# Decode block on one core: one head's softmax ahead of a loop, and the last product in column form

## The chip, the cores and the metric

The kernel runs on one core of a Trainium2 chip. The metric is the device time of one execution in microseconds (us). Three runs of the kernel before gave 355.38, 355.39 and 355.53 us, so its median is 355.39 us. The profile is of a further execution, which took 355.74 us.

## The reference, cut to what matters

One token goes through a block of attention over a cache of keys and values, and then through a feed-forward layer. Both are modulated by a vector c (shift, scale and gate; the rows of `mod` below).

```python
mod = (_silu(c) @ w_mod)                     # sa, ca, ga, sb, cb, gb: 512 numbers each
h = _layernorm(x) * (1 + ca) + sa
x = x + ga * _A_ref(h, k_cache, v_cache, wq, wo)
h = _layernorm(x) * (1 + cb) + sb
x = x + gb * (jnp.maximum(h @ w1, 0) @ w2)

def _A_ref(x, k_cache, v_cache, wq, wo):     # 32 query heads, 8 key/value heads, 32768 positions, Dh = 128
    q = x @ wq
    scores = einsum(q, k_cache) * Dh ** -0.5
    o = einsum(softmax(scores), v_cache)
    return o @ wo
```

All inputs are bf16. The caches are 2 x 64 MB; w_mod is 3 MB, wq and wo are 4 MB each, and w1 and w2 are 1.75 MB each (512 x 1792).

## The kernel before, in words

**Loads.** Every large input goes through a ring of five buffers of 4 MB in SBUF. One queue, SP's, issues all the loads in a fixed order (`stream`, lines 139 to 144): w_mod, wq, the keys of head 0, then in turn half a head's keys of the next head and half a head's values of the current one, at the end the values of head 7 in three parts, wo in four, w1 in two and w2 in six. A load can be issued when its buffer is free again and when the transfer that used its semaphore before has landed.

**Scores.** For a key/value head g, the 32768 positions are four steps (u = 0 to 3) of 64 positions for each of 128 partitions; a load brings two steps. `turn_k` (line 405, VectorE) turns 32x32 blocks of the keys in place, in halves of a step, and `scores` (line 422, TensorE) multiplies them, eight matmuls for a half step, into a PSUM bank that collects two steps. `bank_max` (line 428) copies a full bank to SBUF and takes its maximum.

**Softmax.** `softmax(h)` is a Python generator, so that its pieces can be put between other work; each `next(soft)` emits one piece: (1) the maximum over both banks, `m_p`; (2) its transpose on TensorE, `mT_ps`; (3) `Mrow` and `Mexp` on VectorE; (4) a second transpose `Mb_ps` on TensorE, then on ScalarE `nbias` and the exponentials `P_g`; (5) the turned `PT_g` and `Lexp` on VectorE; (6) the matmul `L_ps`; (7) its reciprocal `Linv`.

**Values.** `pv(g, us)` multiplies the turned P by the values of two steps. For heads 0 to 5, and for the first half of head 6, it is a hardware loop on TensorE (lines 490 to 496), 32 matmuls in eight turns; a loop is a section of its own, and the instructions of all engines are divided by it into those ahead of it and those behind it. The second half of head 6 and all of head 7 are written out. `open_o`, `blocks`, `o_cols` and `normalise` clear, fold, turn and scale a head's output.

**Order.** TensorE's and VectorE's orders are as written (line 599); the other engines' are chosen by the scheduler. The loop of lines 611 to 664 works on two heads: the scores of head h = g + 1 and the values of head g. In its turn g = 5 it does the scores of head 6, piece 1 of head 6's softmax, the loop over the second half of head 5's values, and piece 2. Pieces 3 to 7 stand in the turn g = 6 between the first scores of head 7:

```python
            build_qbd(h)
            turn_k(h, 0, 0); turn_k(h, 0, 1); turn_k(h, 1, 0)     # one a line in the kernel
            scores(h, 0, 0)
            if soft:
                next(soft)
            open_o(g)
            scores(h, 0, 1)
```

**End.** `project` multiplies by wo: its last two parts in column form (lines 566 to 572), where a 128x128 piece of the weights is the stationary operand and one column of the activations moves. Then come the second layernorm and the product with w1 in rows (`hid_ps`, line 714), which is transposed on VectorE (line 724); a ReLU on ScalarE (line 725) spreads it over `hid_bd`, 4x4 diagonal blocks. The product with w2 (line 735) is in row form: the stationary operand is 128x4 of `hid_bd`, 128 columns of w2 move, 56 matmuls, and the result is 4 partitions of 128 numbers. For the last step the gate gb and the residual x1 must lie in the same form; `expand` (line 323) and `four_rows` (line 330) make it, gb near the start (line 340) and x1 inside the second layernorm (`meanwhile`, line 698). `keep_clock(n)` issues n matmuls whose result nobody reads. The output goes from 4 partitions to memory (line 743).

Of the kernel before, what the change touches and what calls it, by code (L numbers as in the profile page):

```python
# [9 lines left out]
BF16 = mybir.dt.bfloat16  # L10
F32 = mybir.dt.float32
ACT = mybir.ActivationFunctionType
ALU = mybir.AluOpType
AX = mybir.AxisListType
# [3 lines left out]
def kernel(  # L18
# [14 lines left out]
    nc = tc.nc  # L33
    P = 128
    _, _, D = A_x.shape
# [3 lines left out]
    KT = D // P  # L39
    Dff = B_w1.shape[1]  # L40
    FT = Dff // P
# [142 lines left out]
    for n in sorted({n * REP for _, n in WOP}):  # L184
# [21 lines left out]
    nc.vector.tensor_reduce(  # L206
        out=place32[:], in_=ident_f[:].rearrange("p (j m) -> p m j", m=32), op=ALU.add, axis=AX.X,
    )
    rowpick = const.tile([P, KT], F32)
    nc.vector.tensor_reduce(  # L210
        out=rowpick[:], in_=ident_f[:].rearrange("p (j m) -> p j m", m=32), op=ALU.add, axis=AX.X,
    )
    hid_bd = const.tile([P, FT, KT, KT], BF16)
    nc.gpsimd.memset(hid_bd[:], 0.0)

    pick8 = const.tile([16, 8], BF16)
    nc.vector.tensor_tensor(out=pick8[:], in0=ident_bf[0:16, 0:8], in1=ident_bf[0:16, 8:16], op=ALU.add)
# [22 lines left out]
    def bank(name):  # L240
        return ps_s.tile([P, 512], F32, tag="s", name=name)[:]
# [75 lines left out]
    for i in range(2):  # L317
# [1 line left out]
            mod_rows[:, i, :].rearrange("q (m ko) -> q ko m", ko=KT),  # L319
            modT_sb[:, 4 * KT * i:4 * KT * (i + 1)].rearrange("p (j ko) -> p j ko", j=4),  # L320
        )

    def expand(src_T, name):
        e = const.tile([P, 32, KT], F32, name=f"{name}_exp")
        nc.vector.tensor_tensor(
            out=e[:], in0=src_T.unsqueeze(1).to_broadcast([P, 32, KT]),
            in1=place32[:].unsqueeze(2).to_broadcast([P, 32, KT]), op=ALU.mult,
        )
        return e

    def four_rows(e, name):

        r_ps = bank(f"{name}_ps")[0:KT, 0:P]
        nc.tensor.matmul(  # L334
            r_ps, lhsT=rowpick[:], rhs=e[:].rearrange("p m kt -> p (m kt)"), start=True, stop=True,
        )
        return r_ps

    gb_rows = const.tile([KT, P], F32)
    nc.scalar.copy(out=gb_rows[:], in_=four_rows(expand(modT_sb[:, 5 * KT:6 * KT], "gb"), "gb"))  # L340

    hT = const.tile([P, KT], BF16)
    stat1 = const.tile([P, 2], F32)
# [35 lines left out]
    def build_qbd(g):  # L379
        d_ap = qbd[g % 2][:]  # L380
        d_ps = d_ap.ap[0][0]
        s_ap = qrep_sb[:]
        s_ps = s_ap.ap[0][0]
        for a in range(4):
            o = AP(d_ap.tensor, d_ap.offset + (32 * a) * d_ps + 4 * 7 + 32 * a,
                   [[d_ps, 32], [QW, 4], [1, 4]])
            i = AP(s_ap.tensor, s_ap.offset + (32 * a) * s_ps + REP * g,
                   [[s_ps, 32], [Hq, 4], [1, 4]])
            nc.scalar.copy(out=o, in_=i)  # L389
# [202 lines left out]
    def keep_clock(n):  # L592

        if not spare:
            spare.append(bank("spare_ps"))
        for _ in range(n):
            nc.tensor.matmul(spare[0], lhsT=ident_bf[:], rhs=qbd[0][:, :, 0:P], start=True, stop=True)  # L597

    with tc.manual_schedule(engines={mybir.EngineType.PE, mybir.EngineType.DVE}):
        build_qbd(0)  # L600
        for u in range(NTILE):
            for half in range(2):
                turn_k(0, u, half)
                scores(0, u, half)
            if u % 2 == 1:
                bank_max(0, u // 2)
        soft = softmax(0)
        for _ in soft:
            pass
        soft = None  # L610
        for g in range(LAST):
            h = g + 1
            build_qbd(h)
            turn_k(h, 0, 0)
            turn_k(h, 0, 1)
            turn_k(h, 1, 0)
            scores(h, 0, 0)
            if soft:
                next(soft)
# [4 lines that stand above are left out]
            if g > 0:  # L624
                blocks(g - 1)
            scores(h, 1, 0)
            if g > 0:
                o_cols(g - 1)
            turn_k(h, 1, 1)
            scores(h, 1, 1)  # L630
            if soft:
                next(soft)
            if g > 0:
                normalise(g - 1)
                if g in [sum(w) for w in WOP]:
                    spread(part_of(g - 1))
            if soft:
                next(soft)
            bank_max(h, 0)
            next(soft or iter(()), None)  # L640
            pv(g, (0, 1))
            for u in (2, 3):
                for half in range(2):
                    turn_k(h, u, half)
                    scores(h, u, half)
            bank_max(h, 1)
            soft = softmax(h)
            next(soft)
            if g < LOOPED:
                pv(g, (2, 3))  # L650
                next(soft)
                continue
            next(soft)
            next(soft)
            pv(g, (2,), range(6))
            next(soft)
            next(soft)
            open_o(LAST)
            pv(g, (2,), range(6, 16))
            pv(g, (3,))  # L660
            next(soft)
            next(soft, None)
            a_rows.append(row_bank("a_ps"))
            blocks(g)
        pv(LAST, (0, 1))
        o_cols(LAST - 1)
        normalise(LAST - 1)
        pv(LAST, (2,))
        spread(2)
        hid_ps = ps_o.tile([P, 512], F32, tag="o", name="hid_ps")  # L670
        nc.vector.memset(hid_ps[:], 0.0)
        pv(LAST, (3,))
        blocks(LAST)
        project(0)
        keep_clock(2)
        o_cols(LAST)
        keep_clock(2)
        project(1)
        normalise(LAST)
        spread(3)  # L680
        keep_clock(2)
        project(2)
        keep_clock(1)
        join_rows()
        keep_clock(2)
        project(3)


        stat2 = const.tile([P, 2], F32)
        x1T = const.tile([P, KT], F32)  # L690
        nc.vector.tensor_tensor(out=x1T[:], in0=attnT_ps, in1=modT_sb[:, 2 * KT:3 * KT], op=ALU.mult)
        nc.vector.scalar_tensor_tensor(
            out=x1T[:], in0=x1T[:], scalar=1.0, in1=xT, op0=ALU.mult, op1=ALU.add, accum_out=stat2[:, 0:1],
        )
        h2T = const.tile([P, KT], BF16)
        x1_ps = []

        def meanwhile():
            e = expand(x1T[:], "x1")
            keep_clock(2)  # L700
            x1_ps.append(four_rows(e, "x1"))
            keep_clock(2)

        keep_clock(3)
        layernorm_T(x1T[:], stat2, h2T[:], modT_sb[:, 3 * KT:4 * KT], ncb[:], "ln2", meanwhile)
        x1_rows = const.tile([KT, P], F32)
        nc.vector.tensor_copy(out=x1_rows[:], in_=x1_ps[0])

        NQ = 32 * FT
        for part, (k0, k1) in enumerate(W1P):  # L710
            w1_sb = need(("w1", part))
            for kt in range(k0, k1):
                for q in range(4):
                    nc.tensor.matmul(  # L714
                        hid_ps[32 * q:32 * q + 1, 0:NQ], lhsT=h2T[:, kt:kt + 1],
                        rhs=w1_sb[:, kt - k0, q * NQ:(q + 1) * NQ], start=False, stop=(kt == KT - 1),
                        skip_group_check=True,
                    )
        keep_clock(3)
        hidT = rows_sb("hidT").rearrange("p a b -> p (a b)")[:, 0:NQ].rearrange("p (f e) -> p f e", e=32)  # L720
        hid_v = hid_ps[:, 0:NQ].rearrange("p (e f) -> p f e", f=FT)
        hb = hid_bd[:]
        for f0, f1 in ((0, FT // 2), (FT // 2, FT)):
            nc.vector.transpose(out=hidT[:, f0:f1], in_=hid_v[:, f0:f1])  # L724
            nc.scalar.activation(
                out=AP(hb.tensor, hb.offset + KT * KT * f0, [hb.ap[0], [KT * KT, f1 - f0], [KT + 1, KT]]),
                in_=hidT[:, f0:f1, 0:1].to_broadcast([P, f1 - f0, KT]), func=ACT.Relu,
            )

        ffn_ps = bank("ffn_ps")[0:KT, 0:P]  # L730
        for part, (f0, f1) in enumerate(W2P):
            w2_sb = need(("w2", part))
            for ft in range(f0, f1):
                for i in range(KT):
                    nc.tensor.matmul(  # L735
                        ffn_ps, lhsT=hid_bd[:, ft, i, :], rhs=w2_sb[:, ft - f0, i * P:(i + 1) * P],
                        start=(ft == 0 and i == 0), stop=(ft == FT - 1 and i == KT - 1),
                    )
        o_rows = const.tile([KT, P], F32)
        nc.vector.tensor_tensor(out=o_rows[:], in0=ffn_ps, in1=gb_rows[:], op=ALU.mult)  # L740
        o_bf = const.tile([KT, P], BF16)
        nc.vector.tensor_tensor(out=o_bf[:], in0=o_rows[:], in1=x1_rows[:], op=ALU.add)
    nc.sync.dma_start(out=out[0, 0].rearrange("(i n) -> i n", i=KT), in_=o_bf[:])


# [28 lines left out]
```

## Time and profile before

| | |
|---|---|
| median of three runs | 355.39 us (355.38 to 355.53) |
| profiled execution | 355.74 us, of which its span, first to last instruction, 353.94 us |
| TensorE matmuls busy | 279.8 us (79%) |
| VectorE busy | 203.1 us (57%) |
| ScalarE busy | 25.4 us (7%) |
| read from memory | 149.42 MB, 422 GB/s over the span |
| mean granted TensorE clock | 0.947 |

PE is TensorE's matmuls, PEld its weight loads, DVE is VectorE, ACT ScalarE, POOL GpSimd, and SPq the queue of the loads; L735 is line 735 of the kernel. A line of the timeline gives the start, the duration, the engine, the line, the operation and the tiles; in brackets stands the engine's idle time before it, and what ended it. A line of the chain of work that ended last gives the start, the duration and the instruction. A line of the windows gives a stretch, its length, the busy time and number of instructions of PE, PEld, DVE, ACT and POOL, the granted clock, the share of time that the transfers were busy, and GB/s.

The transfers are at work from 1.8 us on, and the last piece of w2 lands at 350.5 us. The output's transfer is issued at 351.84 us and has landed at 353.02 us; the rest of the span is the end of the program.

### The profile page before, as it was taken

To read this page: it belongs to the slowest core of one execution; us is meant where nothing else is said; L and a number is where in the kernel's file an instruction comes from. 1 tells how busy PE (TensorE), PEld (TensorE's weight loads), DVE (VectorE), ACT (ScalarE), POOL (GpSimd) and SP (SyncE) were. 2 spreads that over 40 slices of the span, in tenths; PEclk is the share of its full clock that TensorE was granted. 3 is DMA by queue.
4 is the path that set the end of the run, shared out by engine and by line. 5 is a ranking of instruction groups with operands and counts; after the bars stand their busy time and mean duration, and the time that the engine had idled before them with its cause. 6 is when DMAs were issued, how large, how long until landed. Compare 5 with 4: busy or idle time off the path is not lost. (4 is left out here: it accounts for less than half of the span.)

```text
span 353.9 us, 4006 instructions
## 1 busy us (share of the span) xinstructions
PE 279.8 (79%) x1311; PEld 112.7 (32%) x1311; DVE 203.1 (57%) x271; ACT 25.4 (7%) x69; POOL 3.9 (1%) x16
## 2 busy tenths in 40 slices
PE   0542781999898979897979796979689687989996
PEld 0221230333343323332323232323234233334444
DVE  6245775882768268462939178553938095734142
ACT  1220003000010001000100001000100010002000
POOL 4000000000000000000000000000000000000000
PEclk9995997799899999998999899999999997999999
DMA  8999999999999999999999999999999999999994
GB/s 309 455 422 445 431 422 441 441 418 424 459 418 422 459 418 424 441 437 426 433 444 417 430 456 419 427 446 426 422 448 430 422 439 441 422 430 424 421 420 177
DMA packets 6852, 149.59 MB, mean 423 GB/s; under 512 B 824, under 2 KB 1080, under 8 KB 1976
## 3 DMA queue, kind: packets, MB, share of 16 engines
q1 hardware_dynamic: 6776, 149.43, 98.4%
q8 instruction: 8, 0.13, 0.1%
q14 instruction: 4, 0.03, 0.0%
q0 software_dynamic: 64, 0.00, 0.0%
HBM read 149.42 MB, written 0.00 MB: 422 GB/s over the span
## 5 line engine op out<-in xcount | busy, mean ns | idle before, releaser
L405 DVE STREAM_TRANSPOSE Ksb<-Ksb 128x2048 f32<-128x2048 f32 x64 | 142.9, 2281 | 63.9 <-DMA Ksb<-in_A_k_cache_dram 63.9
L484 PE MATMUL o_ps<-Vsb,PT_g 128*16 (+1 forms) x512 | 130.0, 395 | 21.5 <-ACT qbd L389 7.2
L422 PE MATMUL S_ps<-Ksb,qbd 128*128 128x512 bf16 x512 | 121.8, 388 | 23.5 <-DVE Ksb L405 21.9
L422 PEld LDWEIGHTS <-qbd 128*128 128x128 bf16 x512 | 49.0, 98 | 87.6 <-issue 31.8
L484 PEld LDWEIGHTS o_ps<-Vsb,PT_g 128*16 x416 | 37.4, 90 | 90.2 <-issue 63.7
L428 DVE TENSOR_SCALAR_CACHE_REDUCE S_g<-S_ps 128x512 f32<-128x512 f32 x16 | 11.0, 690 | 34.4 <-PE S_ps L422 34.4
L389 ACT COPY qbd<-qrep_sb 32x16 bf16<-32x16 bf16 x32 | 6.4, 201 | 138.7 <-PE S_ps L422 137.6
L465 DVE STREAM_TRANSPOSE PT_g<-P_g 128x1024 bf16<-128x1024 bf16 x8 | 9.7, 1218 | 6.6 <-ACT P_g L459 6.6
L484 PEld LDWEIGHTS <-PT_g 128*16 128x16 bf16 x96 | 8.2, 90 | 11.0
L456 ACT ACTIVATE nbias<-Mb_ps 128x1 f32<-128x1 f32 x8 | 1.4, 171 | 136.8 <-PE Mb_ps L454 136.8
L459 ACT ACTIVATE P_g<-S_g,nbias 128x1024 bf16<-128x1024 f32 x8 | 9.2, 1148 | 0.2
L227 PE MATMUL xc_ps<-cx_sel,cx_bd 16*128 16x2 bf16 x4 | 0.3, 172 | 11.1 <-DVE cx_bd L221 11.1
L515 DVE SCALAR_TENSOR_TENSOR Y<-o_ps,smask,Y 16x128 f32<-16x128 f32 x24 | 8.1, 339 | 0.8
L471 PE MATMUL L_ps<-Lexp,ones_f 128*128 128x4 f32 x16 | 3.0, 257 | 4.3 <-DVE Lexp L468 4.3
L597 PE MATMUL spare_ps<-qbd,ident_bf 128*128 128x512 bf16 x19 | 5.6, 380 | 0.0
L440 PE MATMUL mT_ps<-ident_f,m_p 128*1 128x128 f32 x8 | 2.2, 270 | 3.9 <-DVE m_p L437 2.0
L471 PEld LDWEIGHTS L_ps<-Lexp,ones_f 128*128 128x128 f32 x16 | 3.1, 221 | 5.8 <-issue 5.1
L443 DVE TENSOR_REDUCE Mrow<-mT_ps 1x4 f32<-1x128 f32 x8 | 2.1, 257 | 4.6 <-PE mT_ps L440 4.6
L534 DVE TENSOR_TENSOR oT_sb<-acc_ps,Linv 128x4 bf16<-128x4 f32 x8 | 1.2, 150 | 5.7 <-PE acc_ps L521 5.7
L295 PE MATMUL mod_ps<-wm_sb,siluT 128*1 128x512 bf16 x24 | 3.6, 624 | 1.0 <-DVE siluT L289 1.0
L505 DVE MEMSET o_ps<- 16x512 f32 x8 | 3.9, 485 | 0.8
L552 DVE CAST o_sb<-o_ps 128x4 bf16<-128x4 f32 (+2 forms) x4 | 0.7, 167 | 5.7 <-PE o_ps L548 5.7
(115 smaller groups left out, 80.0 us busy)
## 6 DMA issues: line engine op xcount, KB each, us to landing
Ksb<-in_A_k_cache_dram SPq DMA_DIRECT2D x16, 4096.0 KB, 35.6
Vsb<-in_A_v_cache_dram SPq DMA_DIRECT2D x15, 4096.0 KB, 35.2
wq_sb<-in_A_wq_dram SPq DMA_DIRECT2D x1, 4096.0 KB, 19.6
Vsb<-in_A_v_cache_dram SPq DMA_DIRECT2D x2, 2048.0 KB, 31.8
wm_sb<-in_w_mod_dram SPq DMA_DIRECT2D x1, 3072.0 KB, 10.4
wo_sb<-in_A_wo_dram SPq DMA_DIRECT2D x1, 2048.0 KB, 29.1
w_sb<-in_B_w_dram SPq DMA_DIRECT2D x1, 1344.0 KB
wo_sb<-in_A_wo_dram SPq DMA_DIRECT2D x1, 1024.0 KB, 31.1
```

What stands on the lines that cost most here:

```text
L295: nc.tensor.matmul(dst[j // 4][32 * (j % 4):32 * (j % 4) + 1, :], lhsT=src_T[:, kt:kt + 1], rhs=w[:, kt, j * 512:(j + 1) * 512], start=(kt ...
L389: nc.scalar.copy(out=o, in_=i)
L405: t = nc.vector.transpose(out=KTt.bitcast(F32), in_=KTt.bitcast(F32))
L422: nc.tensor.matmul(S_ps_tiles[g], lhsT=qbd[g % 2][:, hp, 4 * (7 - s):4 * (7 - s) + P], rhs=KTv[:, 16 * sl:16 * sl + 16, h, :, par], start= ...
L428: nc.vector.tensor_scalar(out=S_tiles[g][:, G, :], in0=S_ps_tiles[g], scalar1=1.0, scalar2=None, op0=ALU.mult, op1=ALU.max, accum_out=m_ti ...
L459: nc.scalar.activation(out=P_g[:], in_=S_g[:].rearrange("p g f -> p (g f)"), func=ACT.Exp, bias=nbias[:], scale=scale, accum_out=l_g[:],)
L465: nc.vector.transpose(out=PT_g[:], in_=P_g[:])
L471: nc.tensor.matmul(L_ps[:], lhsT=ones_f[:], rhs=Lexp[:], start=True, stop=True)
L484: nc.tensor.matmul(o_tiles[g][:], lhsT=PT, rhs=Vx, start=False, stop=False, skip_group_check=True)
L505: nc.vector.memset(o_tiles[g][:], 0.0)
L515: nc.vector.scalar_tensor_tensor(out=Y[:], in0=o[:, s], scalar=smask[:, s:s + 1], in1=Y[:], op0=ALU.mult, op1=ALU.add,)
L597: nc.tensor.matmul(spare[0], lhsT=ident_bf[:], rhs=qbd[0][:, :, 0:P], start=True, stop=True)
```

## The change

It has two parts.

The first moves softmax pieces of head 6. In the turn g = 5, pieces 2 to 5 (up to the turned P and `Lexp`) now stand ahead of the loop over the second half of head 5's values, and piece 6 behind it. In the turn g = 6 piece 7 comes right after the turned keys; all four half steps of head 7's first keys are turned first and their scores follow one another.

The second writes the last product in column form. The 128x128 pieces of w2 are stationary, and one column of `hid` (128 x 14) moves, 56 matmuls of one column each into four columns of a PSUM tile that VectorE clears beforehand. The gate and the residual are then used as they are, 128x4. So `expand`, `four_rows`, `rowpick`, `gb_rows`, `x1_rows` and `hid_bd` go; in the layernorm the two pairs of `keep_clock` matmuls with the x1 matmul between them become five `keep_clock` matmuls; the ReLU writes 128x7 twice and not 128x28 twice. The output is stored from 128 partitions, 8 bytes of each, and not from 4 partitions, 256 bytes of each.

```diff
-    rowpick = const.tile([P, KT], F32)
-    nc.vector.tensor_reduce(out=rowpick[:], ...)
-    hid_bd = const.tile([P, FT, KT, KT], BF16)
-    nc.gpsimd.memset(hid_bd[:], 0.0)
...
-    def expand(src_T, name):
-    def four_rows(e, name):
-    gb_rows = const.tile([KT, P], F32)
-    nc.scalar.copy(out=gb_rows[:], in_=four_rows(expand(modT_sb[:, 5 * KT:6 * KT], "gb"), "gb"))
...
+            ahead = h == LAST
             build_qbd(h)
             turn_k(h, 0, 0)
             turn_k(h, 0, 1)
             turn_k(h, 1, 0)
+            if ahead:
+                turn_k(h, 1, 1)
+                next(soft, None)
+                soft = None
             scores(h, 0, 0)
...
             scores(h, 1, 0)
+            if ahead:
+                scores(h, 1, 1)
             if g > 0:
                 o_cols(g - 1)
-            turn_k(h, 1, 1)
-            scores(h, 1, 1)
+            if not ahead:
+                turn_k(h, 1, 1)
+                scores(h, 1, 1)
...
             soft = softmax(h)
             next(soft)
+            if g == LOOPED - 1:
+                for _ in range(4):
+                    next(soft)
             if g < LOOPED:
                 pv(g, (2, 3))
                 next(soft)
...
-        layernorm_T(x1T[:], stat2, h2T[:], modT_sb[:, 3 * KT:4 * KT], ncb[:], "ln2", meanwhile)
-        x1_rows = const.tile([KT, P], F32)
-        nc.vector.tensor_copy(out=x1_rows[:], in_=x1_ps[0])
+        layernorm_T(x1T[:], stat2, h2T[:], modT_sb[:, 3 * KT:4 * KT], ncb[:], "ln2", lambda: keep_clock(5))
+        ffn_ps = bank("ffn_ps")[:, 0:KT]
+        nc.vector.memset(ffn_ps, 0.0)
+        hid = const.tile([P, FT], BF16)
...
+            nc.scalar.activation(out=hid[:, f0:f1], in_=hidT[:, f0:f1, 0], func=ACT.Relu)
...
-                for i in range(KT):
+                for ko in range(KT):
                     nc.tensor.matmul(
-                        ffn_ps, lhsT=hid_bd[:, ft, i, :], rhs=w2_sb[:, ft - f0, i * P:(i + 1) * P],
-                        start=(ft == 0 and i == 0), stop=(ft == FT - 1 and i == KT - 1),
+                        ffn_ps[:, ko:ko + 1], lhsT=w2_sb[:, ft - f0, :].rearrange("p (m ko) -> p ko m", ko=KT)[:, ko, :],
+                        rhs=hid[:, ft:ft + 1], start=False, stop=(ft == FT - 1), skip_group_check=True,
                     )
...
+        o_T = const.tile([P, KT], F32)
+        nc.vector.tensor_tensor(out=o_T[:], in0=ffn_ps, in1=modT_sb[:, 5 * KT:6 * KT], op=ALU.mult)
+        o_bf = const.tile([P, KT], BF16)
+        nc.vector.tensor_tensor(out=o_bf[:], in0=o_T[:], in1=x1T[:], op=ALU.add)
+    nc.sync.dma_start(out=out[0, 0].rearrange("(p k) -> p k", k=KT), in_=o_bf[:])
```

More of the change, by code (lines that the diff above doesn't have):

```diff
@@ L208 @@
     )
-    rowpick = const.tile([P, KT], F32)
-    nc.vector.tensor_reduce(
-        out=rowpick[:], in_=ident_f[:].rearrange("p (j m) -> p j m", m=32), op=ALU.add, axis=AX.X,
-    )
-    hid_bd = const.tile([P, FT, KT, KT], BF16)
-    nc.gpsimd.memset(hid_bd[:], 0.0)
     pick8 = const.tile([16, 8], BF16)
@@ L321 @@
         )
-    def expand(src_T, name):
[L324 to L329, printed above, removed]
-    def four_rows(e, name):
[L333 to L337, printed above, removed]
-    gb_rows = const.tile([KT, P], F32)
-    nc.scalar.copy(out=gb_rows[:], in_=four_rows(expand(modT_sb[:, 5 * KT:6 * KT], "gb"), "gb"))
     hT = const.tile([P, KT], BF16)
@@ L695 @@
         h2T = const.tile([P, KT], BF16)
[L696 to L702, printed above, removed]
         keep_clock(3)
-        layernorm_T(x1T[:], stat2, h2T[:], modT_sb[:, 3 * KT:4 * KT], ncb[:], "ln2", meanwhile)
-        x1_rows = const.tile([KT, P], F32)
-        nc.vector.tensor_copy(out=x1_rows[:], in_=x1_ps[0])
+        layernorm_T(x1T[:], stat2, h2T[:], modT_sb[:, 3 * KT:4 * KT], ncb[:], "ln2", lambda: keep_clock(5))
+        ffn_ps = bank("ffn_ps")[:, 0:KT]
+        nc.vector.memset(ffn_ps, 0.0)
+        hid = const.tile([P, FT], BF16)
         NQ = 32 * FT
@@ L721 @@
         hid_v = hid_ps[:, 0:NQ].rearrange("p (e f) -> p f e", f=FT)
-        hb = hid_bd[:]
         for f0, f1 in ((0, FT // 2), (FT // 2, FT)):
             nc.vector.transpose(out=hidT[:, f0:f1], in_=hid_v[:, f0:f1])
[L725 to L730, printed above, removed]
+            nc.scalar.activation(out=hid[:, f0:f1], in_=hidT[:, f0:f1, 0], func=ACT.Relu)
         for part, (f0, f1) in enumerate(W2P):
@@ L733 @@
             for ft in range(f0, f1):
-                for i in range(KT):
+                for ko in range(KT):
                     nc.tensor.matmul(
-                        ffn_ps, lhsT=hid_bd[:, ft, i, :], rhs=w2_sb[:, ft - f0, i * P:(i + 1) * P],
-                        start=(ft == 0 and i == 0), stop=(ft == FT - 1 and i == KT - 1),
-                    )
[L739 to L743, printed above, removed]
+                        ffn_ps[:, ko:ko + 1], lhsT=w2_sb[:, ft - f0, :].rearrange("p (m ko) -> p ko m", ko=KT)[:, ko, :],
+                        rhs=hid[:, ft:ft + 1], start=False, stop=(ft == FT - 1), skip_group_check=True,
+                    )
+        o_T = const.tile([P, KT], F32)
[3 more added lines that the diff above has]
+    nc.sync.dma_start(out=out[0, 0].rearrange("(p k) -> p k", k=KT), in_=o_bf[:])
 _INS = ['A_x', 'A_k_cache', 'A_v_cache', 'A_wq', 'A_wo', 'B_x', 'B_w1', 'B_w2', 'c', 'w_mod']
```

## The prediction

> **What bounds the kernel now.** I read the page's slices first. Apart from the first and the last, the transfers' row holds nines throughout.
>
> ```profile
> DMA  8999999999999999999999999999999999999994
> ```
>
> So the loads set the pace, and engine time counts only where it ends after the last load it needs. The windows show where that happens:
>
> ```profile
> 320.00:330.00 10.00, 10.00 (x48) 4.25 (x47) 2.89 (x9) 0.46 (x1) 0.00 (x0) 1.00 0.97 413
> ...
> 345.00:350.00 5.00, 4.88 (x63) 2.82 (x62) 1.64 (x7) 0.80 (x3) 0.00 (x0) 1.00 0.82 318
> ```
>
> Towards the end PE (second figure) has no idle time either. PE and the transfers run side by side, and the chain of work that ended last names PE:
>
> ```profile
> 343.25 0.50 PE acc_ps L567 x16
> ...
> 346.10 0.94 PE hid_ps L714 x16
> ...
> 347.89 3.30 PE ffn_ps L735 x56
> ...
> 351.22 0.29 DVE o_rows L740
> ...
> 351.53 0.28 DVE o_bf L742
> ```
>
> The last product takes 3.30 us, 59 ns a matmul by this row, and runs to 351.19. When had its last operand landed? Of SP's loads, the last was issued at 341.81:
>
> ```profile
> L132 SPq DMA_DIRECT2D w_sb<-in_B_w_dram x1: 328/328/328, 341.8 to 341.8; - x1
> ...
> DMA to landing us min/median/max: 8.7/8.7/8.7
> ```
>
> It landed at 350.5, only 0.7 before the product's end. This is the number that decides: whatever PE gains beyond it, the last four matmuls cannot start before 350.5.
>
> The moved softmax lies at 275 us. The timeline there, around the two loops it touches:
>
> ```profile
> 275.82 0.15 DVE L437 TENSOR_REDUCE m_p<-m 128x1 f32<-128x2 f32 x1
> 276.84 0.57 PEld L484 LDWEIGHTS o_ps<-Vsb,PT_g 128*16 x4 [2.29 <-issue]
> 276.87 1.02 PE L484 MATMUL o_ps<-Vsb,PT_g 128*16 x4 [1.82 <-issue]
> ...
> 298.65 8.94 PE L484 MATMUL o_ps<-Vsb,PT_g 128*16 x32 [0.66 <-PE L_ps L471]
> ```
>
> The first loop starts 0.90 after `m_p` ends, though it does not read `m_p`. The list of waits confirms that a loop waits for work whose result it does not use:
>
> ```profile
> PE o_ps L484 <- ACT qbd L389: 7.2, 4, 1.8
> ```
>
> **The change part by part.** The sum is made against the profiled execution: 355.74, span 353.94, 1.80 outside it. The median of the runs is 0.35 lower than that execution.
>
> *Last product.* Row form costs 59 ns a matmul. Column form stands in the trace in the same shape, 128x128 weights and one moving column: L567, 16 in 0.50, 31 ns a pair. So 56 take 1.75 instead of 3.30. Started at 347.89 it would be through at 349.64, but the last piece lands at 350.5. Hence: 350.52 landing, 0.05 until the load starts (as `acc_ps` L521 starts 0.04 after `Y` ends), 0.18 for the first pair (the `o_ps` matmul L548), three more at 0.03, 0.04 to DVE: `o_T` starts at 350.88 instead of 351.22. Gain 0.34, not 1.55. The other 52 pairs need 1.6 and would be done at 349.5, so PE may come 1.05 later than today without moving the end; I call that the slack.
>
> *Last two DVE operations.* 0.28 each in 4x128; in 128x4 the same kind (L691, L692) takes 0.16, starts 0.20 apart. Gain 0.24.
>
> *The store.* Before: issued at 351.84, landed at 353.02, 0.83 after the issue's end; its four 256-byte packets took 15 ns each, and the semaphores landed 0.33 after them. The issue costs the same (0.35; loads of 128 rows 0.33). After: 128 pieces of 8 bytes, eight for each of 16 engines. Nothing in the trace has this shape. From below: no change, as all packets are short (4 bytes: 9 ns), less the 6 ns that each is shorter. Nearest row: the first load of 128 rows, wm, had its first packets 0.65 to 0.91 after its issue, the store 0.43; plus eight packets at 9 ns. From above: eight landings in series, 7 x 0.33 = 2.3. I take +0.2, by the load. The Trainium skill ("DMA: Bandwidth & Descriptors", Specifications) says that transfers below 512 B are read, modified and written; no row here prices that, and it would push towards the upper end.
>
> *ReLU, x1, gb.* The ReLU of 128x28 takes 0.27, the cast of 128x16 (L370) 0.22: 0.05, hidden by the landing. In the layernorm, PE's x1 matmuls (0.31) give way to one more `keep_clock` matmul (0.22), and DVE's `x_exp` and `x_rows` (0.28, 0.27) to a memset of some 0.07. None was on the path: `h2T` ends at 346.03, and w1's last part lands at 346.05 (322.24 plus 23.8), so `hid_ps` could not end much earlier anyway. At the start go `rowpick` (DVE 0.27), `gb_exp` (DVE 0.29), two matmuls (0.38), an ACT copy (0.26) and POOL's last memset (0.30); nothing queues behind the last. wq lands at 20.8 and the first keys at 30.5, and the transfers do not pause: worth nothing. Were that cover gone, it would be 0.3 to 0.6.
>
> *The moved softmax.* Ahead of the loop PE now waits at `Mb_ps` for DVE's `Mrow` and `Mexp`; behind it on PE are the loop's 32 matmuls, `L_ps` and head 7's scores. Head 7's own chain has the durations: `mT_ps` 0.27, `Mrow` 0.28, `Mexp` 0.21. From `m_p` at 275.82 that puts `Mb_ps` at 276.9; with a loop entry of 1.3 (idle before L484: 0.7 to 1.8) the loop starts at 278.3, 1.4 later than now. `P_g` on ACT (1.15) and `PT_g` on DVE (1.25) then run beside it; DVE is free until the keys that it turns at 283.51. PE's longer idle time can bring the half clock: in the windows, 292.23 to 295.65 has PE busy for 1.69 of 3.42, and the next two show a granted clock of 0.50. At half clock a matmul of this loop starts every 0.43, so it can lose up to 2. The loop ends between 287.7 and 289.7 (now 286.28). In return head 7's first scores run as one block: now 286.6 to 297.4 with a gap of 1.73 and the half clock; after, 32 in 7.1 as at 307.78, the last eight not before the fourth turn is through at 292.4. With `o_cols`, `normalise`, `spread` and the entry (2.0) the next loop starts between 297.4 and 299.5; now it does at 298.65. So PE comes to the last heads between 1.2 earlier and 0.9 later. Earlier buys nothing (the landing), later fits the slack. SP's next load waits for the loop's end (286.45) but lands 35.8 after its issue: a delay of 3 is hidden. Worth 0.
>
> *Sum.* -0.34 - 0.24 + 0.2 = -0.38: span 353.56, execution 355.36, median 355.0. No change within 0.2% (0.71 us), which is about what a measurement of this kernel can tell.
>
> **The rivals.**
>
> *The loop waits for the turned P too (slower).* If the loop waits for all that is written ahead of it, as for `m_p` and the qbd copies, it waits for `Lexp`, which in head 7's chain ends 4.9 after `m_p` starts, 0.75 of that spent behind other matmuls. It would start at 280.9, 4.0 later, lose 1 to 2 to the half clock, and the unbroken scores give back 2 to 3: the next loop starts 2.5 to 3.5 late. Above the slack of 1.05, 1.4 to 2.4 reach the end: 356.4 to 357.4. Against: the loop at 298.65 began before `Linv`, written ahead of it, had been waited for in full; `bank_max` was still running at 298.39, 0.03 before its first turn was set up. From a delay of 1.4 on the time is above the old one, from 2.1 on by 0.2%. Chance 0.2.
>
> *The store is dear (slower).* More than 1.1 over the old one, up to 2.3: 355.9 to 357.1. Chance 0.05.
>
> *The transfers end earlier than I count (faster).* 349.96 was when 15 of the 16 engines had delivered the last piece; if the sixteenth keeps up, 0.55 more is gained, and if the store costs nothing extra 0.2 more: 354.3. With no transfer in the way at all the product alone would give 1.55 and the time would be 353.8. Against: the transfers are full from 2 us on, and the amount of data is the same. Chance 0.1.
>
> *Column form is no faster than row form.* At 59 ns a pair it ends where it did; 0.24 less, 0.2 more: 355.4. L567 speaks against it. Chance 0.05.
>
> *The weight loads do not overlap (slower).* One 128-column load takes 118 ns (L567, median); 56 in series are 6.6, 3.3 more than now: 358.6. The row refutes it: those loads start every 31 ns. Chance 0.02. The Trainium skill ("TensorE: Matmul & The Clock Gate", LDWEIGHTS) gives the columns over 1.2 as a load's nanoseconds, 107 for 128, against 3 for the 4 columns of today; by that alone 56 would be an estimated 6.0 and the time an estimated 358.0. The trace agrees with the duration and not with such a sum.
>
> **How the numbers follow.** My forecast has 0.58, its own range 354.7 to 355.7 (the store without an extra, or with one of 0.9). Faster: 0.1. Slower: 0.2 + 0.05 + 0.02 = 0.27. Within 0.2%: 0.58 + 0.05 = 0.63. The range goes from 354.4 to 357.0: it takes in most of the earlier landing, and half of the late loop.
>
> **What would show it.** Right: `ffn_ps` in groups with idle time between them, released by w2's loads; the last four starting just after 350.5; `o_T` and `o_bf` at 0.16; the store 0.83 to 1.1 after its issue. The loop over head 5's second half starts near 278.3 and `PT_g` runs beside it. Wrong: that loop starts only after `Lexp`, near 281, and `ffn_ps` is one unbroken row ending after 351.2; or the last load lands well before 350; or the store lands later than 1.5 after its issue.

## The result

The changed kernel takes 356.66 us (356.50 to 357.07), the kernel before on the same chip 355.42 us (355.29 to 355.53). The ratio is 1.0035, with a 95% interval of 1.0024 to 1.0047: 1.24 us slower. The prediction was 355.0 us and no change; the time lies inside its range, on the side to which it gave 0.27.

The profiled execution after took 356.75 us, its span 354.97, which is 1.03 longer than the span before. The transfers' row of the slices is as full as it was:

```profile
DMA  8999999999999999999999999999999999999993
```

The windows, as before, for the long middle and for the last product (length, then busy time of PE, PEld, DVE, ACT, POOL, the granted clock, the transfers' share, GB/s):

```profile
320.00:330.00 10.00, 10.00 (x47) 4.08 (x45) 2.34 (x7) 0.00 (x0) 0.00 (x0) 1.00 0.98 416
345.00:350.00 5.00, 4.09 (x70) 2.46 (x69) 1.15 (x5) 0.43 (x2) 0.00 (x0) 1.00 0.83 321
```

In the last stretch PE now has 0.9 us of idle time where it had 0.1. What it waits for stands in PE's list of waits (total, times, longest), and the chain that ended last agrees:

```profile
PE ffn_ps L709 <- DMA w_sb<-in_B_w_dram: 0.7, 2, 0.4
```

```profile
341.59 8.70 DMA w_sb<-in_B_w_dram
...
350.33 0.31 PE ffn_ps L709 x4
...
350.66 0.17 DVE o_T L714
...
350.86 0.16 DVE o_bf L716
```

So up to the last sum the change loses nothing: the last piece of w2 lands at 350.29, four matmuls follow, and the store is issued at 351.05, 0.79 us earlier than before. The loss is behind that. Below are the store's issue in the kernel before, its issue and landing in the changed kernel, and then SP's wait for it at the end, first in the kernel before and then in the changed one (the numbers behind DMA_DIRECT2D are the issue's duration in ns and its start):

```profile
L743 SPq DMA_DIRECT2D out_dram<-o_bf x1: 348/348/348, 351.8 to 351.8; - x1
```

```profile
L717 SPq DMA_DIRECT2D out_dram<-o_bf x1: 347/347/347, 351.1 to 351.1; - x1
...
DMA to landing us min/median/max: 3.0/3.0/3.0
```

```profile
SPq L769 <- DMA out_dram<-o_bf: 0.4, 1, 0.4
```

```profile
SPq L743 <- DMA out_dram<-o_bf: 2.2, 1, 2.2
```

The issue takes 0.35 in both. The last semaphore comes 2.65 us after the issue's end where it came 0.83 after it: 1.82 more. The 128 packets themselves were quick: all went out between 351.89 and 352.09, at 7 to 9 ns each. The first of the sixteen engines' semaphores landed at 352.30, the others one by one until 354.05.

In the experiments "the landing" is always the last semaphore, counted from the end of the store's issue and read from the trace of one execution. For the changed kernel's store, 128 pieces of 8 B side by side in the output, it scatters: 2.65 here, 2.30 and 2.53 in two kernels below.

### The profile page after: what moved, and what is told of

The parts are those of the page before. It is cut to its first block, busy times and chain, and to the rows that moved or that the text cites. A ratio compares the mean times of both kernels' runs of the same rounds, so it can differ in the third digit from the quotient of the medians.

```text
span 355.0 us, 3993 instructions
## 1 busy us (share of the span) xinstructions
PE 279.6 (79%) x1308; PEld 111.4 (31%) x1308; DVE 202.0 (57%) x268; ACT 25.1 (7%) x68; POOL 3.7 (1%) x15
## 5 line engine op out<-in xcount | busy, mean ns | idle before, releaser
L337 PE MATMUL q_ps<-wq_sb,hT 128*1 128x512 bf16 x32 | 3.6, 627 | 2.5 <-DMA wq_sb<-in_A_wq_dram 2.5
```

What stands on the lines that cost most here:

```text
L337: nc.tensor.matmul(q_ps[i][32 * a:32 * a + 1, :].rearrange("o (h e) -> o h e", e=32), lhsT=hT[:, kt:kt + 1], rhs=wq_f[:, kt, i, a], start= ...
```

## The experiments

**One part alone.** First the softmax move without the column form. This kernel is the changed one with the end of the kernel before:

```diff
-    nc.sync.dma_start(out=out[0, 0].rearrange("(p k) -> p k", k=KT), in_=o_bf[:])
+    nc.sync.dma_start(out=out[0, 0].rearrange("(i n) -> i n", i=KT), in_=o_bf[:])
```

together with `expand`, `four_rows`, `hid_bd` and the row form of the product, as in the diff's removed lines.

> The first part of the change alone: head 6's softmax ahead of the loop, with the row form and the old store. Theory (the loss is all in the store of 128 pieces of 8 bytes, the rest of the change is a gain): PE reaches the layernorm some 0.6 us earlier, as in the changed kernel (h2T ended at 345.40 instead of 346.03), the row-form product starts near 347.3 and would end 3.3 later, held up a little by the last landing near 350.4; the store, landed 0.83 after its issue as before, is issued 0.3 to 0.6 us earlier: 354.9 to 355.2. Rival (moving the softmax costs time of its own): 355.5 or more.

Measured: 355.41 us (355.13 to 356.24) against 355.24 (354.97 to 355.73), ratio 1.0005 [0.9996, 1.0014]. No difference is measured, and the gain that was expected is not seen. In its trace the last product begins 0.70 earlier than in the kernel before (347.19, was 347.89), but now it has to wait for the transfers too. The wait in PE's list, and the part of the chain behind the wait:

```profile
PE ffn_ps L746 <- DMA w_sb<-in_B_w_dram: 0.2, 1, 0.2
```

```profile
349.02 1.74 PE ffn_ps L746 x28
```

The second half of the product starts when a piece of w2 has landed (348.98) and ends at 350.76, 0.44 earlier than before. Whether these 0.44 us are in the time is not settled: the interval reaches from 0.14 faster to 0.50 slower.

Then the column form and its store without the softmax move, the second part of the diff alone:

> The second part alone: column form and the store from 128 partitions, softmax where it was. Theory: the end hangs on the last landing, and PE coming 0.6 us later stays inside the slack of 1.05, so the time is that of the changed kernel, 356.5 to 356.8, with a store that lands 2.6 us after its issue's end. Rival (part of the loss is the softmax): clearly below 356.5, by what the softmax costs.

Measured: 356.59 us (356.57 to 356.97), ratio 1.0039 [1.0025, 1.0053], the changed kernel's loss. Its landing is 2.30, and the wait at its end:

```profile
SPq L732 <- DMA out_dram<-o_bf: 1.9, 1, 1.9
```

So the second part holds the whole loss.

**The store with fewer and larger pieces.** The changed kernel, with its last sum and store on `NP` partitions:

```diff
-        o_bf = const.tile([P, KT], BF16)
+        o_bf = const.tile([NP, D // NP], BF16)
...
-    nc.sync.dma_start(out=out[0, 0].rearrange("(p k) -> p k", k=KT), in_=o_bf[:])
+    nc.sync.dma_start(out=out[0, 0].rearrange("(i n) -> i n", i=NP), in_=o_bf[:])
```

> The changed kernel with the old shape of the store, 4 partitions of 256 bytes; the last addition takes its operands from the first 4 partitions and repeats them, so the output does not hold the block's result, and the addition is of 4x128 (0.28 us instead of 0.16). Theory: the store lands 0.83 us after its issue again and the time is 356.66 - 1.82 + 0.12 = 354.96, between 354.8 and 355.2. Rival (something else at the end is slow, the store only shows it): 356.5 or more.

> As the store from 4 partitions, but from 16 partitions of 64 bytes, one piece for each of 16 engines (the output again does not hold the block's result; the addition is of 16x32). It tells pieces from engines. Theory (each of the 128 small pieces adds some 14 ns one after another in memory, 1.75 us in all): 16 pieces add 0.2, landed 0.8 to 1.1 after the issue's end, 354.8 to 355.2. Rival (16 engines, each with its own semaphore update, are what is slow): landed 2.6 after the issue's end, 356.5 or more.

Measured with 4 pieces of 256 B: 355.06 us (354.88 to 355.33), ratio 0.9994 [0.9984, 1.0003], landing 0.83. With 16 pieces of 64 B: 355.20 (354.88 to 355.24), ratio 0.9993 [0.9984, 1.0003], landing 0.99. SP's last wait, for 4 and for 16 pieces:

```profile
SPq L747 <- DMA out_dram<-o_bf: 0.4, 1, 0.4
```

```profile
SPq L747 <- DMA out_dram<-o_bf: 0.6, 1, 0.6
```

Apart from the last sum (0.28 us with 4 pieces, 0.18 with 16, 0.16 in the changed kernel) these kernels are the changed kernel, so the 1.2 us vanish with the shape of the store. Sixteen engines, each with its own semaphore, cost 0.16 of landing; they are not the cause. That leaves the number of pieces, their size, or where they lie.

**Number, size or place.** Here the final store goes to a scratch tensor in memory, `far`, whose rows lie a chosen distance apart; a store of x in bf16, issued early from POOL's queue, takes the output's place.

```diff
+    x_bf = const.tile([P, KT], BF16)
+    nc.vector.tensor_copy(out=x_bf[:], in_=xT)
+    nc.gpsimd.dma_start(out=out[0, 0].rearrange("(p k) -> p k", k=KT), in_=x_bf[:])
...
-    nc.sync.dma_start(out=out[0, 0].rearrange("(p k) -> p k", k=KT), in_=o_bf[:])
+    far = nc.dram_tensor("far", [P, 32], BF16, kind="Internal").ap()
+    nc.sync.dma_start(out=far[:, 0:4], in_=o_bf[:])
```

Rows of 32 elements are 64 B apart; 2048, 16 and 4 elements make 4 KB, 32 B and 8 B. For the wide pieces, each partition repeats its sum over the whole row and stores all of it (`far[:, 0:32]`, `far[:, 0:256]`).

> The changed kernel with its last store, still 128 pieces of 8 B, sent to a scratch tensor of the device's memory whose rows are 64 B apart; the block's result is left out (the output gets x in bf16, stored early). In the changed kernel the sixteen semaphores came between 0.91 and 2.65 us after the end of the issue, in the kernel with sixteen pieces of 64 B between 0.82 and 0.99, with four of 256 B at 0.83. Theory A, each small write takes its turn wherever it goes (1.75 us / 128 = 14 ns; the sixteen pieces' spread of 0.17 us / 16 = 11 ns agrees): as in the changed kernel, last landing 2.2 to 2.7 after the issue's end, time 1.2 above the kernel before. Theory B, the pieces of one 64 B stretch of memory get in each other's way (eight pieces of 8 B lie in each, written by different engines): here each piece has its stretch to itself, last landing 0.9 to 1.1, time 0.3 below the kernel before to equal.

> As the run with rows 64 B apart (the block's result is left out in the same way), the 128 pieces of 8 B now 4 KB apart. Theory A: last landing 2.2 to 2.7 after the issue's end. Theory B with stretches of 64 B: 0.9 to 1.1, as 64 B apart. If the stretch that is shared is longer than 64 B (up to 4 KB), 64 B apart stays slow and this one lands at 0.9 to 1.1.

> As the run with rows 64 B apart (the block's result is left out in the same way), each of the 128 partitions now writing 64 B, its own whole row of the scratch tensor: same number of pieces, no stretch of 64 B shared or written in part. Theory A (a turn for each write): 2.2 to 2.7 after the issue's end. Theory B: 0.9 to 1.1. Theory C, a part of a longer stretch costs a read and a write of the whole (the Trainium skill, DMA: Bandwidth & Descriptors, Specifications, has such a rule for pieces below 512 B): 2.2 to 2.7, since 64 B are still far below 512 B.

> As before (the block's result is left out in the same way), each of the 128 partitions writing its own row of 512 B. Theory A (a turn for each write): 2.2 to 2.7 after the issue's end, and more if the turn grows with the bytes. Theory B and theory C: 0.9 to 1.3 (64 KB over sixteen engines, 8 pieces each, at about 25 ns a piece by a straight line through 8 ns for 8 B and 15 ns for 256 B: 0.2 us of packets instead of 0.07). Together with the run of 64 B rows it tells a rule on 512 B (slow there, fast here) from a turn for each write (slow in both) and from a shared stretch (fast in both). The last sum writes 256 elements a partition instead of 4, so its own instruction is longer; only the landing after the issue's end is read.

> As the run with rows 64 B apart (the block's result is left out in the same way: the output gets x in bf16, stored early), the rows of the scratch tensor now 8 B apart, so that eight pieces of 8 B share each stretch of 64 B, as in the output of the changed kernel. It asks whether the scratch tensor itself is what makes the landing early. If pieces that share a stretch hinder each other: last landing 2.2 to 2.7 after the issue's end, as in the changed kernel (2.65) and in the column form alone (2.30). If the scratch tensor is another kind of memory: 1.0 to 1.1, as with 64 B apart (1.07).

> As the run with rows 64 B apart (the block's result is left out in the same way), the rows now 32 B apart: two pieces in each stretch of 64 B. If the stretch that matters is 64 B, by the excess of the eight sharers (1.2 to 1.6 us over the 1.07 of no sharer, shared out over seven later pieces, so 0.17 to 0.23 each): last landing 1.2 to 1.4. If it is 32 B or less: 1.07 as with 64 B apart.

| 128 pieces of | from start to start | landing, us |
|---|---|---|
| 8 B | 8 B | 2.45 |
| 8 B | 32 B | 1.06 |
| 8 B | 64 B | 1.07 |
| 8 B | 4 KB | 1.07 |
| 64 B | 64 B | 1.06 |
| 512 B | 512 B | 1.19 |

SP's last wait with rows 8 B apart, and with rows 64 B apart:

```profile
SPq L747 <- DMA far<-o_bf: 2.0, 1, 2.0
```

```profile
SPq L747 <- DMA far<-o_bf: 0.6, 1, 0.6
```

Theory A falls: 128 small writes do not take turns of 14 ns, since 128 of the same size land at 1.07 when they lie apart. Theory C falls as well: pieces of 8 B that lie apart and pieces of 64 and 512 B, which fill their rows and so touch each other, differ by 0.13 at most. The scratch tensor is no special memory, as rows 8 B apart show (2.45). What is left is theory B, that pieces disturb each other by being close together; but not any two pieces in 64 B do so, since rows 32 B apart, two in each 64 B, cost nothing.

These kernels as a whole were slower than the last store can explain: they took 356.81 to 358.58 us. With rows 64 B apart a time at most equal to the kernel before was expected, and it was 357.23 us, ratio 1.0049 [1.0033, 1.0065], in spite of its early landing. That has its own experiment, further down.

**Who writes the neighbour.** The first kernel deals the pieces to other places of the output: partition 16 b + a writes row 8 a + b.

```diff
-    nc.sync.dma_start(out=out[0, 0].rearrange("(p k) -> p k", k=KT), in_=o_bf[:])
+    nc.sync.dma_start(out=out[0, 0].rearrange("(a b k) -> b a k", a=16, k=KT), in_=o_bf[:])
```

> The changed kernel with its store's pieces dealt to other places of the output: partition 16 b + a writes to row 8 a + b, so that neighbours among the partitions write 64 B apart, and each stretch of 64 B is written by the partitions a, 16 + a, 32 + a, ... (the result comes out in another order, which leaves the block's own order out). Number and size of the pieces, and the 1 KB that they fill, stay. If what costs is that pieces written one right after another meet in a stretch, and partitions sixteen apart go to the same engine: last landing 0.9 to 1.4, time 0.2 to 0.5 below the kernel before. If every piece of a shared stretch waits for the one before, whoever writes it and when: 2.2 to 2.7, time 1.1 to 1.4 above.

Measured: 357.52 us (357.43 to 357.81), ratio 1.0062 [1.0039, 1.0085], landing 2.91. SP's last wait:

```profile
SPq L743 <- DMA out_dram<-o_bf: 2.5, 1, 2.5
```

The other order does not help; both the landing and the time, 2.2 above the kernel before, are beyond either expectation. In the profiled execution the store has landed 1.06 later than in the changed kernel: 0.40 because the last piece of w2 landed later, 0.41 because the issue took 0.75 and not 0.35, and 0.25 behind the issue. But the trace shows eight engines' semaphores here and not sixteen: the store went out as eight rows of sixteen pieces. The count of engines follows the outer of the two dimensions. If each row's pieces went to one engine, which the count suggests and no trace shows, every piece still had neighbours from other engines. The opposite can be written as well, sixteen rows of eight pieces that fill 64 B each:

```diff
-    far = nc.dram_tensor("far", [P, 32], BF16, kind="Internal").ap()
-    nc.sync.dma_start(out=far[:, 0:4], in_=o_bf[:])
+    far = nc.dram_tensor("far", [16, 64], BF16, kind="Internal").ap()
+    nc.sync.dma_start(out=far[:, 0:32].rearrange("a (b k) -> a b k", k=KT), in_=o_bf[:])
```

> As the runs with the scratch tensor (the block's result is left out: the output gets x in bf16, stored early). The 128 pieces of 8 B go as sixteen groups of eight, each group filling its own 64 B, the groups 128 B apart; written as sixteen rows of eight pieces, so that each row's pieces should go to one transfer engine (in the run with the store dealt in another order, eight rows of sixteen pieces used eight engines). Theory D, pieces of one stretch hinder each other where different engines write them: last landing 1.0 to 1.3 after the issue's end. Theory E, each piece of a shared stretch waits for the one before, whoever writes it: eight in a row, 2.2 to 2.7 (2.45 with rows 8 B apart).

Measured: landing 1.22, sixteen semaphores.

```profile
SPq L747 <- DMA far<-o_bf: 0.8, 1, 0.8
```

Eight pieces of 8 B that touch each other can thus be harmless, and theory E falls. What made them so is less certain. Theory D, that one engine writes each row, forecast the time. But the traces do not show which engine writes which piece, neither here nor in the changed kernel's store of 128 rows, and this kernel changed something else as well: it left 64 B free behind every 64 B. That touching pieces of 8 B are late only where they fill more than 64 B without a gap fits the runs too. A store of sixteen rows of eight pieces without gaps would tell the two apart; it was not run.

**How close is too close.** Two kernels with pieces of 32 and 16 B in the real output, 32 and 64 partitions in the edit of the second group:

> The changed kernel with its last sum and store on 32 partitions, 32 pieces of 32 B; the output is filled with the values of the first 32 partitions, repeated, so most of the result is left out. If only pieces that share 32 B or less hinder each other: last landing 0.95 to 1.1 after the issue's end (sixteen pieces of 64 B: 0.99; 128 of 8 B, 32 B apart: 1.06). If the number of pieces in 1 KB counted: 0.83 + 32 x 14 ns = 1.3.

> As the run with 32 pieces, on 64 partitions: 64 pieces of 16 B, two in each stretch of 32 B (most of the result is left out in the same way). If the stretch is 32 B: two sharers wait for each other, 1.2 to 1.6 after the issue's end (the excess of 1.4 to 1.6 of the four sharers, shared out over three later pieces, 0.47 to 0.53 each, above 0.99 would be 1.46 to 1.52). If it is 16 B or less: 0.95 to 1.1.

Measured: landing 1.00 with 32 pieces (354.92 us in a single run, before 355.31) and 1.17 with 64 pieces (355.53 in a single run). The 1.17 lies between the two expectations. The traces show where its 0.17 above the 32 pieces lie: 0.15 of them pass before the first packet, which starts 0.65 after the issue's end and not 0.50. From the first packet on the two need 0.52 and 0.50, so touching pieces of 16 B do not hinder each other in this run.

Three more kernels deal the pieces as the other order did, on eight engines (with neighbours that belong to different engines, if each row has its own), at three distances:

```diff
-    nc.sync.dma_start(out=far[:, 0:4], in_=o_bf[:])
+    nc.sync.dma_start(out=far.rearrange("(a b) w -> b a w", a=16)[:, :, 0:4], in_=o_bf[:])
```

> As the runs with the scratch tensor (the block's result is left out: the output gets x in bf16, stored early). The 128 pieces of 8 B go out in the dealing of the run in another order (eight rows of sixteen pieces, on eight engines; neighbours in memory belong to different engines), to rows 64 B apart, so that none shares 64 B. If only sharing costs: last landing 1.1 to 1.4 after the issue's end (1.22 with sixteen engines that each own their stretch; sixteen pieces an engine now). If this dealing is slow by itself: 2.3 to 2.9 (2.91 with all 128 in 1 KB).

> As the run before it, the rows 32 B apart: two pieces of different engines in each 64 B. If the stretch is 64 B: later than with 64 B apart by 0.15 or more (the 64 pieces of 16 B, four in each 64 B, came 0.17 later than the 32 of 32 B; eight sharers cost 1.4 to 1.7). If it is 32 B or less: as with 64 B apart, within 0.05.

> As the run before it, the rows 16 B apart: four pieces of different engines in each 64 B, two in each 32 B. If the stretch is 64 B: clearly between none and eight sharers, 1.5 to 2.3. If it is 32 B: two sharers each, later than with 32 B apart by 0.15 or more. If it is 16 B: as with 64 B apart.

Measured: 1.17, 1.17 and 1.16. SP's last wait with rows 16 B apart:

```profile
SPq L747 <- DMA far<-o_bf: 0.7, 1, 0.7
```

So eight engines in this dealing are not slow by themselves, and the 2.91 was due to the pieces' distance. That two pieces in one stretch of 64 or of 32 B hinder each other is refuted, unless it only costs from more than four pieces in 64 B on, or unless the eight rows are not dealt one to an engine. The shortest distance that landed early is 16 B; 8 B is late. That a stretch of 16 B is what two engines may not share fits all of these runs if neighbours in the store of 128 rows belong to different engines; neither that nor the 16 B as a unit of the hardware was shown.

**What the colliding pieces do to other transfers.** In the scratch kernels the early store of x is itself a store of 128 pieces 8 B apart. This kernel is the changed one, whole, with the same early store to rows 64 B apart:

```diff
+    x_bf = const.tile([P, KT], BF16)
+    nc.vector.tensor_copy(out=x_bf[:], in_=xT)
+    far = nc.dram_tensor("far", [P, 32], BF16, kind="Internal").ap()
+    nc.gpsimd.dma_start(out=far[:, 0:4], in_=x_bf[:])
```

> The changed kernel, whole, with one store more: x in bf16, 128 pieces of 8 B, goes early to a scratch tensor with rows 64 B apart, from the queue and at the time at which the scratch runs stored it to the output, 8 B apart. There the second transfer of weights (wq) landed 22.5 to 23.0 us after the start and 11.5 to 11.9 after the first, in the changed kernel 20.74 and 9.63: 1.9 to 2.3 later, and the kernels' ends with it. Theory F, the pieces that share a stretch hold up the engines and the weights behind them: without sharers wq lands 9.6 to 9.9 after the first transfer, and the time is the changed kernel's, 1.1 to 1.6 above the kernel before. Theory G, any early store of 128 pieces costs that: wq 11.5 to 11.9 after the first, time 2.8 to 3.4 above the kernel before.

Measured: 356.95 us (356.59 to 356.97), ratio 1.0042 [1.0022, 1.0061], 1.64 us above the kernel before (355.31), just over the 1.6 that was expected, and within its interval the changed kernel's own loss (its last store landed at 2.53). The transfer behind the early store is that of wq, 4 MB. Its landing in the list of transfers (size, us from issue to landing), in the scratch kernel with rows 64 B apart and the early store 8 B apart, and in this kernel:

```profile
wq_sb<-in_A_wq_dram SPq DMA_DIRECT2D x1, 4096.0 KB, 21.7
```

```profile
wq_sb<-in_A_wq_dram SPq DMA_DIRECT2D x1, 4096.0 KB, 19.8
```

The windows from 19 to 21 us, when the early store is under way (the last two figures are the transfers' share and GB/s), show where the time goes, in the scratch kernel with rows 8 B apart and in this one:

```profile
19.00:21.00 2.00, 0.00 (x0) 0.00 (x0) 0.69 (x5) 0.00 (x0) 0.00 (x0) 0.87 0.15 33
```

```profile
19.00:21.00 2.00, 0.06 (x1) 0.00 (x0) 1.26 (x7) 0.00 (x0) 0.00 (x0) 1.00 1.07 459
```

With colliding pieces the weights all but stop, 33 GB/s, and with the same pieces apart they run on at 459. In the ten kernels with the early store 8 B apart these 2 us show 0 to 197 GB/s. The weights' own packets show it too: those of 32 KB took at most 1.21 us around this time in the changed kernel and here, and up to 3.2 to 3.9 us in each of the ten. Counted from the first transfer's landing, wq landed 11.5 to 11.9 us later in the six scratch kernels of the table, 11.6 to 12.5 in the other four, 9.63 in the changed kernel and 9.71 here. Theory F holds. It also explains the scratch kernels' times: with an end like that of the kernels with few pieces, the one with rows 64 B apart was 1.7 us slower than before (357.23 against 355.54), because a kernel bound by its transfers pays a stop of 1.9 us at 20 us as it does at the end.

No kernel here was measurably faster than the kernel before: the column form with the cheapest store (4 pieces) is between 0.6 us faster and 0.1 us slower than the kernel before, and it leaves out putting the result into rows.

## Why the prediction was wrong

**What bounds the kernel: right.** The transfers' row stays full, and the last load ends the chain together with the few matmuls that need it.

**Last product: right.** The four last matmuls started just after the landing, and `o_T` 0.37 after it (0.36 forecast). Measured from before, `o_T` is 0.56 earlier: 0.33 by the product (0.34 forecast), and 0.23 because the last piece landed at 350.29 and not at 350.52. No run shows that the change caused those 0.23. The same landing was at 350.27 with the softmax move alone, at 350.48 with the column form alone, at 350.38 and 350.41 with 4 and 16 pieces, and at 350.69 in the kernel that only stores in another order; it scatters by more than that. The idle time between the groups shows that the 31 ns a matmul of the nearest row and the bound by the landing were both needed. Column form "no faster" and loads that do not overlap are refuted.

**Last two DVE operations: right.** 0.16 each, and 0.39 from the start of `o_T` to the store's issue, 0.62 before: 0.23 gained, 0.24 forecast.

**ReLU, x1, gb: right.** None of them appears in the chain after, and wq landed as it did (20.74, before 20.78).

**The moved softmax: right in its times.** The timeline of the changed kernel:

```profile
275.58 0.15 DVE L412 TENSOR_REDUCE m_p<-m 128x1 f32<-128x2 f32 x1
...
278.30 8.24 PE L459 MATMUL o_ps<-Vsb,PT_g 128*16 x28 [1.32 <-issue]
278.50 1.25 DVE L440 STREAM_TRANSPOSE PT_g<-P_g 128x1024 bf16<-128x1024 bf16 x1 [1.79 <-ACT P_g L434]
...
298.00 2.53 PE L459 MATMUL o_ps<-Vsb,PT_g 128*16 x8 [1.58 <-DVE S_g L403]
```

The loop started at 278.30 (278.3 forecast) with `PT_g` beside it, so the rival in which it waits for the turned P is refuted. It ended at 287.7, the early end of the forecast; the half clock came (granted clock 0.57 from 279 to 283 us) and did not cost more than the forecast allowed for. The next loop started at 298.00, inside 297.4 to 299.5. From there on PE was some 0.6 ahead, and in column form this buys nothing, because the landing ends the chain. That the move is worth nothing agrees with the two runs that differ by it: 1.0039 [1.0025, 1.0053] without it and 1.0035 [1.0024, 1.0047] with it.

**The store: wrong; this is the step that failed.** Its term was +0.2 and measured +1.82. The sum was -0.34 - 0.24 + 0.2; measured in the profiled execution it is -0.56 - 0.23 + 1.82 = 1.03, the whole difference of the spans. (With the other two landings of this store, 2.30 and 2.53, the term would be 1.47 and 1.70.) The prediction took the value "by the load", the first load of 128 rows. That row has the right number of pieces and says nothing about where they end: a load's pieces go to 128 partitions, the store's lie side by side in 1 KB of memory. The pieces 64 B apart show what the forecast was in effect about: 1.07, against 0.83 + 0.2 = 1.03.

The rival "the store is dear" came true in its time, 355.9 to 357.1, and the sign named for it, a landing later than 1.5 after the issue, was there. Its mechanism did not: eight landings in series for an engine would make any 128 pieces late, and 128 pieces 32 B or more apart landed at 1.06 to 1.07. That the time agrees is luck. That the time lies inside the forecast's range is luck too: the range's upper end was set for half of the late loop, and the loop was not late. The rival had been given 0.05, and the prediction names no row against it; a bound of 2.3 from above with nothing against it deserved more.

The prediction also named the Trainium skill ("DMA: Bandwidth & Descriptors", Specifications), by which transfers below 512 B are read, modified and written. It pushed in the right direction, but the runs show no price that follows that limit: 128 pieces of 8 B 64 B apart landed at 1.07, 128 of 64 B at 1.06, 128 of 512 B at 1.19.

## What to carry to other kernels

A store is judged by what it leaves in memory, not only by its packets: 128 pieces of 8 B from as many partitions that ended up side by side landed 1.2 to 1.8 us later than the same pieces 16 B or more apart. Touching pieces of 16 B and more were early as well. When a result is turned from a few rows into a column over 128 partitions, its last store is part of the price, and at the end of a kernel nothing hides it. Such a store in the middle of a kernel bound by transfers is not hidden either, because it stops the loads behind it.

## What the runs showed of the hardware

- 128 touching pieces of 8 B, 1 KB in all: 2.30 to 2.91 us from the end of the issue to the landing, in the output and in a scratch tensor; 1.06 to 1.07 at distances of 32 B to 4 KB on sixteen engines, 1.16 to 1.17 at 16 to 64 B on eight; 1.22 for sixteen groups of eight touching pieces with gaps of 64 B between them. That it is the meeting of different engines that costs was not shown. The store's packets took 7 to 9 ns in the slow case too, so their durations do not show the collision; the landing of the semaphores does.
- While they collide, other transfers of the core nearly stop: 0 to 197 GB/s in a stretch of 2 us, packets of 32 KB that took up to 3.2 to 3.9 us and not 1.21, and the weights behind them landed 1.9 to 2.9 us later in ten kernels.
- The number of engines followed the store's outer dimension: eight semaphores for eight rows of sixteen pieces, sixteen for sixteen rows of eight. The Trainium skill ("DMA: Bandwidth & Descriptors", Why a DMA increments its semaphore by 16 and not by 1) says that the engines are the largest number up to 16 that divides the slowest dimension of both sides; the traces agree.
- The issue of a store with two dimensions of pieces took 0.62 to 0.75 us, with one dimension 0.33 to 0.36 (but 0.55 with 64 pieces of 16 B).
